# Two transposing filter loads, placed later on SyncE's queue, in a two-layer SSM-convolution and GeGLU kernel

## The chip, the cores and the metric

The kernel runs on one core of one Trainium2 chip. The metric is the device time of one execution in microseconds, the median of several runs; lower is better. Engines are named as in the profile: PE is TensorE's matmul, PEld its weight load, DVE is VectorE, ACT is ScalarE, POOL is GpSimd, SP is SyncE, which here only issues DMA transfers.

## What is computed

The input x has 2048 tokens of 576 values in bf16. Two layers follow each other, each a gated long convolution and a GeGLU feed-forward block, with the same weights in both layers:

```python
x = A_q
x = x + _A_ref(_layernorm(x), A_k, A_v, A_shift_k, A_ssm_k, A_ssm_D)
x = x + _B_ref(_layernorm(x), B_w_gate, B_w_up, B_w_down)
x = x + _A_ref(_layernorm(x), A_k, A_v, A_shift_k, A_ssm_k, A_ssm_D)
x = x + _B_ref(_layernorm(x), B_w_gate, B_w_up, B_w_down)
```

`_A_ref(q, ...)` forms kv, a four-tap causal filter of k times v, convolves every channel of kv along the tokens with its filter ssm_k of 2048 taps (576 rows in memory, one per channel), adds kv times a constant and multiplies by q. `_B_ref` is (gelu(x w_gate) * (x w_up)) w_down with an inner width of 4608.

## The kernel before, in words

**Chunks and units.** Tokens are cut into four chunks of 512. A unit is one layer of one chunk. The convolution of a chunk doesn't depend on x and is computed once for both layers; it is done by blocks of 512 taps, so that chunk m needs the filter blocks 0 to m. Block b of ssm_k must be turned, since it lies channel by channel in memory and the matmuls want taps on partitions. Blocks 0 and 1 are loaded plainly (tile hn) and turned by PE (L1251). Blocks 2 and 3 are turned by the DMA itself: `natural(b)` (L1082) issues one transposing load from memory into half of a tile nat (L1086, 128 x 4 x 576 bf16, 576 KB) and then a store of that half into a memory buffer hs[b] (L1087). hs[2] and hs[3] are read by POOL's loads L239, at 124.3 and 312.0 us in the profile. The tile nat is one of two buffers of the pool "x" (tag x); the other holds x_c[0], the fp32 residual of chunk 0. x_c[1], first written by a gate at L892, needs a buffer of this pool.

**The set-up** (L1089 to L1479) prepares chunk 0: kv, the first convolution, the layernorms, and the turned rows xnT of unit (0,0). Its steps are tasks of a planner (`Plan`, L72): `add(engine, cost, function, dependencies)` enters a task; `order` simulates the engines, and the tasks are emitted by planned start. SP's tasks form the list `loads`, made a strict sequence by `chain` (L1464): x's first chunk, the filter block 1, gate/up tiles 0 and 1, `natural(2)`, gate/up tile 2. `load_x(1)`, the load of x's second chunk into the single buffer x_b (pool xbp), is a POOL task (L1472) after `pluses`, the four gates on DVE (L1394) that read x's first chunk out of that buffer.

The end of the set-up, for each of the four row groups j of chunk 0: ACT makes yh (L1385), DVE gates (L1394), ACT squares (L1411, with an accumulator read), POOL makes ve and rstd (L1419, L1420), DVE normalises to xn (L1427), PE turns xn (L1439, L1441), DVE or ACT copies the turned rows to xnT (L1446, L1449). Forty filler matmuls (L1366) run on PE in the wait. Then the first gate/up matmuls start in halves of their columns (L1008, tile ps in the profile). Beside its roots, POOL issues the loads of k's and v's second chunk (L229, L234) and stores the transformed filter and kv blocks (Hd at L1270, Kd at L1296).

**After the set-up** (L1483) SP gets the w_down tiles 0 and 1, `natural(3)`, and w_down tile 2. Then the loop over visits runs (L1500): a visit is a third of the inner width for one unit, 12 gate/up tiles (4 tiles of weights per load, so three loads a visit) and then four groups of down matmuls (L1577). Between the tiles, `fill` works off the convolution of later chunks by costs. Gate/up weights stand in three buffers: the load of group n+3 is queued when group n is used up. Each engine and each DMA queue works in the order of emission.

Of the kernel before, what the change touches and what calls it, by code (L numbers as in the profile page):

```python
# [25 lines left out]
FG = 4  # L26
# [45 lines left out]
class Plan:  # L72
# [8 lines left out]
    def add(self, eng, cost, run=None, deps=(), lat=0.0, bank=False, frees=(), ready=0.0, prio=0.0):  # L81
        task = Task(eng, cost, run, [d for d in deps if d is not None], lat, bank, list(frees), ready, prio)
        for b in task.frees:
            b.users += 1
        self.tasks.append(task)
        return task
# [607 lines left out]
def ssm_geglu_kernel(ctx, tc, A_q, A_k, A_v, A_shift_k, A_ssm_k, A_ssm_D, B_x, B_w_gate, B_w_up,  # L694
                     B_w_down, out):
    nc = tc.nc
# [42 lines left out]
    def run_late(limit):  # L739
        if not late or late[0][0] > t.pe or max(t.dve, t.pe - 1.0) + C_EVD > limit:  # L740
            return False
        add_late()
        return True
# [42 lines left out]
    def load_wd(n):  # L786
        if n >= NWB * 2:
            return
        r0 = (n % (NP * 2)) * WT * P
        d = dpool.tile([P, WT, D], BF16, tag="wd", name="wd")  # L790
        nc.sync.dma_start(out=d[:], in_=B_w_down[r0:r0 + WT * P, :].rearrange("(ft p) d -> p ft d", p=P))
        wd[n] = d

    def load_x(c, eng=None):
        x_b[c] = xbp.tile([P, RT, D], BF16, name=f"x_b{c}", tag="xb")
        (eng or nc.gpsimd).dma_start(out=x_b[c][:],
                                     in_=q2[c * CH:(c + 1) * CH, :].rearrange("(p j) d -> p j d", j=RT))
        xb_at[c] = t.pe + 8.0
# [175 lines left out]
    def run_vq(limit):  # L974
        if not vq:
            return False
        need, cost, run = vq[0]
        if isinstance(need, float):
            r = need
        elif need[0] == "v":  # L980
            r = need[1].get(need[2], NEVER)
        else:
            r = NEVER if len(xn_made) >= 3 or not xn_open() else need[1].get("rstd_at", NEVER)
        if r > t.pe + 0.2 or max(t.dve, t.pe - 1.0) + cost > limit:
            return False
        vq.popleft()
        run()
        t.on_dve(cost, r)
        return True
# [3 lines left out]
    def spreads(now=False, tensor=False):  # L993
        while xn_made and (now or xn_made[0][3] <= t.pe):
            if tensor and xn_made[0][0] == ahead[1] and t.pe > ahead[0] - SLOW and conv.ps_free[0] <= t.pe:
                turn_row(*xn_made.popleft())
                continue
            ui, j, xn, _, entry = xn_made.popleft()
            entry[0] = True
            if j == 0:  # L1000
                xnT_of[ui] = xtp.tile([P, NKC, CH], BF16, tag="xnT", name="xnT")
            spread(xnT_of[ui], j, xn)
            xn_done[ui] = j + 1
# [37 lines left out]
    def when_due(when, load, n):  # L1041
        due.append((when, len(due), load, n))
        due.sort(key=lambda d: d[0])

    def weights():

        while due:
            near = xn_made or (vq and isinstance(vq[0][0], tuple) and vq[0][0][0] == "xn")
            if near and due[0][0] > t.pe + HOLD:
                break  # L1050
            _, _, load, n = due.pop(0)
            load(n)
# [3 lines left out]
    def pressing():  # L1056

        ui = coming[0]
        return (ui is not None and xn_done.get(ui, 0) < RT and units[ui][1] in conv.z_at and bool(vq)
                and t.pe > due_at[0] - PRESS)  # L1060

    def fill(limit, tensor, conv_first):
        weights()
        conv.run_loads()
        spreads(tensor=tensor)
        while True:
            if run_late(limit):
                continue
            if conv_first:
                if not (conv.run_v(limit) or run_vq(limit)):  # L1070
                    break
            elif not (run_vq(limit) or not pressing() and conv.run_v(limit)):
                break
        run_aq(min(limit, t.pe + 2.3))
        if tensor:
            for _ in range(3):
                if pressing() and (units[coming[0]][1], RT - 1) in conv.y_at or not conv.run_p():
                    break
# [3 lines left out]
    def natural(b):  # L1082
        if not nat:
            nat.append(xpool.tile([P, 2, RT, D], BF16, tag="x", name="nat"))
        h = nat[0][:, b - 2, :, :]
        nc.sync.dma_start_transpose(out=h, in_=A_ssm_k[:, b * BS:(b + 1) * BS])  # L1086
        nc.sync.dma_start(out=conv.hs[b].rearrange("(r p) d -> p r d", p=P), in_=h)  # L1087

    with tc.manual_schedule():  # L1089
# [5 lines left out]
        add = plan.add  # L1095
        with ExitStack() as es:
# [48 lines left out]
            def chain(tasks):  # L1145
                for a, b in zip(tasks, tasks[1:]):
                    b.deps.append(a)
# [135 lines left out]
            for m in KTS:  # L1283
                K0[m] = []
                for s in range(2):
                    def fill_ps(task, m=m, s=s):
                        if s == 0:
# [4 lines left out]
                                           prio=-4.0 * KTS.index(m)))  # L1292
# [71 lines left out]
            def busy():  # L1364
                for _ in range(4):
# [5 lines left out]
            loads = [add("SP", 0.6, lambda: load_x(0, nc.sync)),  # L1371
                     add("SP", 1.2, lambda: hn.__setitem__(1, load_hn(1)))]
# [7 lines left out]
            early_xn, pluses, copies = [], [], {}  # L1380
# [77 lines left out]
            for n in range(3):  # L1458
                loads.append(add("SP", 2.0, lambda n=n: load_wgu(n), [[], [], t0][n]))
                loads[-1].lat = 6.0  # L1460
                if n == 1:
                    loads.append(add("SP", 6.0, lambda: natural(2)))
            wg0 = loads[2]
            chain(loads)  # L1464
            add("ACT", 1.28, lambda: nc.scalar.activation(out=warm[:], in_=conv.pis[:], func=ACT.Gelu_apprx_tanh), [tsin], prio=20.0)
            for fi in range(2):
# [2 lines left out]
                    turn[fi] = task.slot  # L1469
                    gu_half(early[fi], fi, 0)  # L1470
                later(lambda me: add("PE", 0.99, me(half_of), early_xn[0] + early_xn[1] + [wg0], bank=True, prio=0.0))
            add("POOL", 0.6, lambda: load_x(1), pluses, prio=-50.0)  # L1472
            order = plan.order({"DVE": 1.9, "ACT": 3.3, "PE": 3.0, "POOL": 3.0, "SP": 4.5})
            for task in order:
                task.run()
# [4 lines left out]

        hpool = pool("hT", 1)
        dpool = pool("wd", 3)
        for n in range(2):  # L1483
            load_wd(n)
        natural(3)
        load_wd(2)
        conv.step(1, loaded=True)
        conv.left = len(conv.V)
        for m in range(2, NCH):
# [10 lines left out]
        for at, (wb, ph, ui, first, final) in enumerate(visits):  # L1500
# [33 lines left out]
            for fi in range(FP):  # L1534
                n, gi = divmod(wb * FP + fi, FG)
                w = wgu[n]
                if wb == 0 and fi in early:
                    pair = early.pop(fi)
                    taken[0] += 1
                    gu_half(pair, fi, 1)  # L1540
                    t.pe = max(t.pe, free.popleft()) + C_GU / 2
                else:
                    pair = pr("gu")
                    gu(pair, w, gi, lambda a: a, xnT)
                    t.pe = max(t.pe, free.popleft()) + C_GU
                while run_late(NEVER):
                    pass
                if hurry() and t.act <= t.pe + 0.2:
                    ga = work.tile([P, 2, CH], BF16, tag="ga", name="ga")
                    nc.scalar.activation(out=ga[:, 0, :], in_=pair[:, 0, :], func=ACT.Gelu_apprx_tanh)  # L1550
                    nc.scalar.copy(out=ga[:, 1, :], in_=pair[:, 1, :])  # L1551
                    nc.vector.tensor_tensor(out=hT[:, fi, :], in0=ga[:, 0, :], in1=ga[:, 1, :], op=ALU.mult)  # L1552
                    there = t.on_act(2 * C_GELU, max(t.pe + 0.15, gone[0]))
                    gone.append(t.on_dve(C_HB, there + 0.15) + 0.1)
                    free.append(there + 0.1)
                    bank_at[taken[0] % 3] = free[-1]
                    lead = FAR
                else:
                    ga = work.tile([P, CH], F32, tag="ga", name="ga")
                    nc.scalar.activation(out=ga[:], in_=pair[:, 0, :], func=ACT.Gelu_apprx_tanh)  # L1560
                    nc.vector.tensor_tensor(out=hT[:, fi, :], in0=ga[:], in1=pair[:, 1, :], op=ALU.mult)  # L1561
                    gone.append(t.on_dve(C_HT, t.on_act(C_GELU, max(t.pe + 0.15, gone[0])) + 0.15) + 0.1)
                    free.append(gone[-1])
                    bank_at[taken[0] % 3] = free[-1]
                    lead = LEAD
                if gi == FG - 1 and final:
                    when_due(t.pe + (FP - FG) * C_GU + 12.0, load_wgu, n + 3)
                fill(t.pe + C_GU + lead, hurry(), conv.left > 0)
            ahead[:] = [t.pe + RT * FP * C_DN, visits[at + 1][2] if at + 1 < len(visits) else None]
            for j in range(RT):  # L1570
# [105 lines left out]
```

## Time and profile before

| | us |
|---|---|
| median of 3 timed runs (937.97, 940.51, 940.17) | 940.17 |
| profiled execution | 937.94 |
| its span, first to last instruction | 936.2 |
| PE busy in the span | 920.4 |
| DVE / ACT / POOL busy | 580.1 / 325.7 / 140.3 |
| mean granted clock of TensorE | 0.994 |

All times of instructions below count from the start of the span. In the lines of the timeline the first number is the start, the second the duration, both in microseconds; after them come engine, line and operation, the tile written and the tile read, and in brackets the idle time of the engine before it with what ended it. A q behind an engine's name is its queue: an instruction that issues a transfer. The duration of such an instruction is how long the engine was busy issuing; the time from issue to landing is shown in the views of a tile and of the DMA queues. In the chain of waits, "issue" is time in which the profile shows nothing that was waited for.

### The profile page before, as it was taken

Reading aid. Unit: us, or ns where it says so; the run is one execution under the profiler, and the core shown is the slowest. Engines: PE = TensorE matmul, PEld = TensorE weight load, DVE = VectorE, ACT = ScalarE, POOL = GpSimd, SP = SyncE. Lnnn points to the kernel's source line nnn. Section 1 sums busy time; section 2 is a strip of 40 time slices with the busy share of each in tenths; the row PEclk is TensorE's granted clock in tenths of the full one; section 3 lists DMA queues with packets and bytes.
Section 4 is the critical chain, followed back from the end, with each engine's and each line's share of the span. In section 5 each row is a group of like instructions: output and inputs, shape, how many; then the busy total and the mean of one; then the engine's idle time right before and its main releaser. Section 6 shows DMA issues by size and latency. Waiting matters only on the chain.

```text
span 936.2 us, 19163 instructions
## 1 busy us (share of the span) xinstructions
PE 920.4 (98%) x8103; PEld 531.9 (57%) x8103; DVE 580.1 (62%) x1109; ACT 325.7 (35%) x594; POOL 140.3 (15%) x306
## 2 busy tenths in 40 slices
PE   9799999999999999999999999999999999999998
PEld 6555565665655646646556556556556556556555
DVE  7667677778788899758988973553333334533332
ACT  7546426553323136353222322451221214411211
POOL 3213200422012203230111200130000002100000
PEclk9989999999999999999999999999999999999999
DMA  9999998525934910891962920691630630696630
GB/s 234 144 249 234 309 243 186 138 52 167 222 119 91 262 48 2 171 310 40 217 191 75 190 78 26 102 204 26 130 99 2 128 102 14 121 221 152 147 70 27
DMA packets 125307, 129.69 MB, mean 139 GB/s; under 512 B 39714, under 2 KB 117411, under 8 KB 125220
## 3 DMA queue, kind: packets, MB, share of 16 engines
q1 hardware_dynamic: 115874, 92.33, 47.6%
q0 software_dynamic: 9200, 35.54, 12.3%
q8 instruction: 63, 1.03, 0.5%
q10 hardware_dynamic: 146, 0.59, 0.2%
q14 instruction: 24, 0.20, 0.1%
HBM read 108.09 MB, written 11.80 MB: 128 GB/s over the span
## 4 chain that ended last, share of the span: by engine, by line
PE 95%; DVE 2%; ACT 1%; issue 1%; POOL 1%; DMA 0%; ACTq 0%; DVEq 0%; SPq 0%
PE gu L1008 60%; PE dn L1577 28%; PE ps L281 1%; PE cps L290 1%; PE cps L343 1%; PE ps L1008 1%; PE ps L1218 1%; DVE kc L602 1%; PE cps L301 0%; PE ps L1340 0%; PE ps L1251 0%; DVE ab L308 0%; DVE cd L308 0%; ACT eo L303 0%; DMA xnT<-xn 0%
## 5 line engine op out<-in xcount | busy, mean ns | idle before, releaser
L1008 PE MATMUL gu<-xnT,wgu 64*128 64x512 bf16 x5148 | 561.1, 376 | 2.2 <-DVE x_c L1619 1.5
L1008 PEld LDWEIGHTS <-wgu 64*128 64x128 bf16 x5220 | 256.0, 94 | 305.2 <-issue 9.6
L1560 ACT ACTIVATE ga<-gu 128x512 f32<-128x512 f32 x256 | 152.8, 597 | 471.3 <-PE gu L1008 465.2
L1561 DVE TENSOR_TENSOR hT<-ga,gu 128x512 bf16<-128x512 f32 x256 | 175.6, 686 | 204.1 <-ACT ga L1560 202.6
L1577 PE MATMUL dn<-wd,hT 128*128 128x288 bf16 x2304 | 294.1, 286 | 0.0
L1577 PEld LDWEIGHTS <-hT 128*128 128x128 bf16 x2304 | 223.5, 98 | 65.4 <-issue 9.3
L840 POOL TENSOR_SCALAR means<-s 128x1 f32<-128x1 f32 x28 | 11.8, 422 | 239.9 <-DVE x_c L1613 205.3
L1621 DVE TENSOR_TENSOR x_c<-x_c,dn 128x576 f32<-128x576 f32 x32 | 24.1, 752 | 30.9 <-PE dn L1577 30.9
L1619 DVE SCALAR_TENSOR_TENSOR x_c<-dn,means,x_c 128x576 f32<-128x576 f32 x28 | 22.7, 815 | 26.8 <-PE dn L1577 26.7
L856 POOL TENSOR_TENSOR rstd<-ve,neghalf_t 128x1 f32<-128x1 f32 x56 | 35.5, 635 | 4.7
L320 DVE TENSOR_TENSOR prod<-prod 128x576 bf16<-128x576 bf16 x72 | 33.0, 458 | 2.5
L1550 ACT ACTIVATE ga<-gu 128x512 bf16<-128x512 f32 x30 | 17.9, 597 | 44.1 <-PE gu L1008 43.0
L303 ACT ACTIVATE eo<-cps 128x576 f32<-128x576 f32 x32 | 20.4, 649 | 25.0 <-DVE ab L308 9.8
L418 POOL DMA_DIRECT2D kr<-Kd x24 | 13.2, 550 | 87.3 <-DVE prod L319 86.1
L1600 DVE TENSOR_TENSOR xn<-x_c,dn 128x576 bf16<-128x576 f32 x15 | 11.3, 753 | 24.0 <-PE dn L1577 23.9
L602 DVE TENSOR_TENSOR kc<-ab,cd 128x288 bf16<-128x288 f32 x64 | 25.7, 451 | 0.0
L422 POOL DMA_DIRECT2D hr<-Hd x36 | 19.4, 540 | 41.1 <-DVE prod L319 39.5
L1552 DVE TENSOR_TENSOR hT<-ga 128x512 bf16<-128x512 bf16 x31 | 13.1, 422 | 18.5 <-ACT ga L1551 18.5
L840 POOL TENSOR_SCALAR nm<-s 128x1 f32<-128x1 f32 x28 | 8.7, 312 | 99.8 <-DVE x_c L892 99.7
L848 ACT ACTIVATE junk<-x_c,nm 128x576 bf16<-128x576 f32 x28 | 21.5, 767 | 4.9 <-POOL nm L840 4.9
L882 ACT ACTIVATE yh<-y,rstd 128x576 f32<-128x576 bf16 x28 | 21.4, 768 | 2.3 <-POOL rstd L856 2.3
L855 POOL TENSOR_SCALAR ve<-ss 128x1 f32<-128x1 f32 x56 | 15.3, 273 | 42.9 <-ACT junk L848 42.8
(170 smaller groups left out, 612.8 us busy)
## 6 DMA issues: line engine op xcount, KB each, us to landing
wgu<-in_B_w_gate_dram SPq DMA_DIRECT2D x45, 576.0 KB, 6.1
wd<-in_B_w_down_dram SPq DMA_DIRECT2D x30, 864.0 KB, 8.0
wgu<-in_B_w_up_dram SPq DMA_DIRECT2D x45, 512.0 KB, 8.2
hr<-Hd POOLq DMA_DIRECT2D x36, 288.0 KB, 7.8
kr<-Kd POOLq DMA_DIRECT2D x24, 288.0 KB, 6.6
Kd<-kc POOLq DMA_DIRECT2D x12, 288.0 KB, 6.4
k<-in_A_k_dram POOLq DMA_DIRECT2D x3, 1008.0 KB, 11.8
wgu<-in_B_w_up_dram SPq DMA_DIRECT2D x45, 64.0 KB, 8.0
```

What stands on the lines that cost most here:

```text
L320: nc.vector.tensor_tensor(out=dst[:, cols], in0=pr[:, 0, cols], in1=pr[:, 1, cols], op=ALU.subtract if part == 0 else ALU.add)
L602: nc.vector.tensor_tensor(out=into[k][:, plane, cols], in0=a, in1=b, op=op)
L840: nc.gpsimd.tensor_scalar(out=v["nm"][:], in0=v["s"][:], scalar1=-1.0 / D, scalar2=None, op0=ALU.mult)
L848: nc.scalar.activation(out=junk[:], in_=get_x(), func=ACT.Square, bias=v["nm"][:, 0:1], accum_out=v["ss"][:])
L856: nc.gpsimd.tensor_tensor(out=v["rstd"][:], in0=ve[:], in1=neghalf_t[:, 0:1], op=ALU.pow)
L882: nc.scalar.activation(out=g["yh"][:], in_=conv.y[c][:, j, :], func=ACT.Identity, scale=g["rstd"][:, 0:1], bias=1.0)
L1008: nc.tensor.matmul(cols(pair[:, s, :]), lhsT=w[r0:r0 + HK, k, gi * P:(gi + 1) * P], rhs=cols(xnT[r0:r0 + HK, blk_of[k], :]), start=(k == 0 ...
L1560: nc.scalar.activation(out=ga[:], in_=pair[:, 0, :], func=ACT.Gelu_apprx_tanh)
L1561: nc.vector.tensor_tensor(out=hT[:, fi, :], in0=ga[:], in1=pair[:, 1, :], op=ALU.mult)
L1577: nc.tensor.matmul(acc[:, h, 0:HW], lhsT=hT[:, fi, j * P:(j + 1) * P], rhs=wd[2 * wb + fi // WT][:, fi % WT, h * HW:(h + 1) * HW], start=( ...
L1619: nc.vector.scalar_tensor_tensor(out=xh, in0=acc[:, :, 0:HW], scalar=m_[:, 0:1], in1=xh, op0=op, op1=ALU.add)
L1621: nc.vector.tensor_tensor(out=xh, in0=xh, in1=acc[:, :, 0:HW], op=ALU.add)
```

## The change

Three moves on the DMA queues; no arithmetic is touched.

- In the set-up, `natural(2)` goes from between gate/up tiles 1 and 2 to the end of SP's sequence.
- `load_x(1)` goes from POOL to SP, behind gate/up tile 2 and ahead of `natural(2)`. It still waits for the four gates (`pluses`).
- `natural(3)` goes from between the w_down tiles 1 and 2 into the first visit, behind the matmuls of its ninth gate/up tile (`fi == 2 * FG`, FG = 4). The three w_down loads now stand together.

```diff
             for n in range(3):
                 loads.append(add("SP", 2.0, lambda n=n: load_wgu(n), [[], [], t0][n]))
                 loads[-1].lat = 6.0
-                if n == 1:
-                    loads.append(add("SP", 6.0, lambda: natural(2)))
             wg0 = loads[2]
+            loads.append(add("SP", 0.6, lambda: load_x(1, nc.sync), pluses, prio=-50.0))
+            loads.append(add("SP", 0.1, lambda: natural(2)))
             chain(loads)
...
-            add("POOL", 0.6, lambda: load_x(1), pluses, prio=-50.0)
             order = plan.order({"DVE": 1.9, "ACT": 3.3, "PE": 3.0, "POOL": 3.0, "SP": 4.5})
...
-        for n in range(2):
+        for n in range(3):
             load_wd(n)
-        natural(3)
-        load_wd(2)
         conv.step(1, loaded=True)
...
                     when_due(t.pe + (FP - FG) * C_GU + 12.0, load_wgu, n + 3)
+                if wb == 0 and fi == 2 * FG:
+                    natural(3)
                 fill(t.pe + C_GU + lead, hurry(), conv.left > 0)
```

## The prediction

> **What bounds the kernel.** Page, parts 1 and 2 first: TensorE (PE) is busy 98% of the span, so only time in which PE waits or runs at a lower clock can be won. The list of waits by engine gives PE 6.1 us in one wait, for DVE xn L1427, and under 1.6 us in every other. It lies in the set-up. The chain of waits there:
>
> ```profile
> 37.63 0.04 issue
> 37.67 2.41 PE ps L1366 x40
> 40.08 3.16 issue
> 43.24 0.28 POOL v L234
> 43.52 0.49 issue
> 44.01 0.54 POOL Kd L1296
> 44.55 0.02 issue
> 44.57 0.25 POOL ve L1419
> 44.82 0.07 issue
> 44.89 0.57 POOL rstd L1420
> ...
> 51.45 3.96 PE ps L1008 x36
> 55.41 1.00 PE ps L1251 x10
> ```
>
> PE ends its filler matmuls (L1366) at 40.08 and has nothing to do: the rows xn of chunk 0 need rstd, and POOL makes rstd only after it has issued two transfers at 43.24 and 44.01. The squares that rstd needs were there long before: ACT's first accumulator read (L1411) ends at 36.25, the last at 39.99. So POOL is what is late. Its timeline:
>
> ```profile
> 28.87 0.54 POOL L1270 DMA_DIRECT2D Hd<-h  x1 [1.43 <-ACT h L1267]
> 43.24 0.54 POOL L234 DMA_DIRECT2D v<-in_A_v_dram  x1 [13.83 <-issue]
> 44.01 0.54 POOL L1296 DMA_DIRECT2D Kd<-kc  x1 [0.23 <-issue]
> ```
>
> For 13.83 us POOL stands before the load of v's second chunk. The buffer of v was free at 29.9 (PE's last L275). What fits is another landing: that load is POOL's ninth transfer; the first, k's second chunk, was issued at 16.23 and by its tile's view took 26.4 us, so it landed at 42.6, 0.6 before v was issued. POOL's tenth transfer (Kd, 44.01) follows the landing of the second (Hd, 18.49 + 25.0 = 43.5) by 0.5. POOL does not issue a transfer while the one eight before it is in flight. And k was slow because of its neighbour on SyncE's (SP's) queue:
>
> ```profile
> 10.92 2.79 SPq L783 DMA_DIRECT2D wgu<-in_B_w_up_dram  x1
> 13.76 26.94 SPq L1086 DMA_TRANSPOSE nat<-in_A_ssm_k_dram  x1
> 51.12 0.40 SPq L1087 DMA_DIRECT2D hs<-nat  x1
> ...
> 57.31 11.32 SPq L1086 DMA_TRANSPOSE nat<-in_A_ssm_k_dram  x1
> 70.61 0.38 SPq L1087 DMA_DIRECT2D hs<-nat  x1
> ```
>
> The transposing load of filter block 2 (576 KB) holds SP 26.94 us and lands after 37.3; that of block 3 takes 11.32 and 13.3 (the two landings have the median 25.3 on the page). Beside the first ran k and seven stores of Hd and Kd (288 KB each, landing after 21.6 to 25.0 us, or up to 23.8); beside the second POOL issued nothing. The page's median for k's loads from POOL is 11.8 us. The last view is the busy time by stretches (PE, PEld, DVE, ACT, POOL, then PEclk, DMA share, GB/s):
>
> ```profile
> 42.00:44.00 2.00, 0.00 (x0) 0.00 (x0) 0.00 (x0) 0.00 (x0) 0.54 (x1) 1.00 1.09 193
> 46.00:48.00 2.00, 1.87 (x16) 1.36 (x16) 1.08 (x3) 0.43 (x1) 1.83 (x5) 0.50 1.31 88
> 52.00:54.00 2.00, 2.00 (x22) 1.46 (x20) 0.25 (x1) 0.00 (x0) 0.00 (x0) 0.50 1.02 398
> 56.00:58.00 2.00, 2.00 (x29) 1.42 (x29) 0.76 (x1) 0.20 (x1) 0.00 (x0) 1.00 1.14 202
> ```
>
> After the idle time the granted clock is 0.50 from about 45 to 55: the hole is paid twice.
>
> **The change, part by part.**
>
> *Block 2's transposing load leaves 13.76.* In its place SP issues the third gate/up tile (1152 KB), whose buffer is free since PE's L1251 at 9.4. No trace shows k beside that tile. From below, k takes the median 11.8 and lands at 28.0; from above it takes 26.4 as now. The nearest rows are the gate/up pieces issued up to 13.8, which land after 11.5 to 19.6; with the longest, k lands at 35.8. I take about 33. Between k's landing and the first root stand 0.6 to v, v 0.54, 0.23, Kd 0.54: 1.9 us. The first square is there at 36.25, so k costs nothing up to 34.4, and after that a microsecond for each.
>
> *The rows then.* The first rstd can be made from 36.3 and xn follows 0.92 after its ve (44.57 to 45.49), but DVE's last gate ends at 39.1: xn at 39.1 to 39.7. The last square (39.99) and roots 1.04 apart put the fourth xn at 41.5 to 42.1. PE's filler ends at 40.06; the transposes need banks that ACT's two copies of y (39.89, 1.16 long) free at 40.5 and 41.05. So the first of four turns starts at 40.6. A turn is 10 transposes, 1.04 us at full clock (L1251 at 36.45); four take 4.2, and the gate/up halves start at 44.8 instead of 51.39: **6.6 us**. Without the wait for banks it would be 7.1; with turns as slow as now (46.13 to 51.39, 5.26) 5.5.
>
> *The clock.* PE's pause shrinks from 6.07 us to about half a microsecond, so I expect no drop. The first 36 half matmuls, 3.96 us in the chain, then cost what the later 18 cost at full clock (1.09), twice: 2.18. **1.8 us**; nothing if the clock drops all the same.
>
> *Load of x's second chunk, POOL to SP.* On POOL it stood behind the roots (48.53, 0.63): nothing is gained there. On SP it waits for DVE's last gate, which frees x_b, until 38.9; behind it stand block 2's load, its store, the three w_down tiles and the next gate/up tiles. It lands 7.1 to 7.3 later, before now.
>
> *Block 2 at 39.5.* No row shows it beside x_b, v and Kd, the neighbours it may meet. From below 13.3 us as block 3, from above 37.3. POOL issues no transfer of its own then until the Hd stores (73.20 now, some 65 then), so the nearer row is 13.3: landed at 52.8. Then the store, and the first w_down tile at 53.3, landing after 7.3 to 15.0: 68.3 at the latest. The first down matmul (82.72) is due at 82.72 - 8.4 = 74.3. Hidden, with 6 us to spare.
>
> *Block 3 behind the ninth tile.* It takes 11.32 us of SP out from before the third w_down tile and stands behind the fifth gate/up tile (waiting for tile 8's release, 73.4 - 8.4 = 65.0, and 6.4 to issue): 71.4. Landing at 84.7 by its own row; behind it waits the sixth gate/up tile, issued at 85.1 and landing 15.7 later (median of set-up pieces), 100.8. It is due at the ninth tile of the next visit, 99.12 + 8 x 1.95 - 8.4 = 106.3. Hidden by 5.5 us. Its store is read at 312. The tile nat shares its slots with x_c; the next x_c is first written at 161.17, long after.
>
> Sum: 6.6 + 1.8 = **8.4 us** (5.5 to 8.9). From 51.45 to 168 the chain runs through PE alone and PE's later waits are 1.5 us at most, fed by PE's own results; the rest should shift as a whole. The profiled execution took 937.94 (span 936.2): 929.5. The median of the three timed runs, 940.17, lies 2.2 above it; with half of that I forecast **931**.
>
> **The rivals.**
>
> *k still late* (0.12): the wide gate/up tile holds k beyond 34.4. For it: it has twice the bytes of nat, and no row shows the pair. Against: k's own median 11.8. With k at 37 to 40, 2.6 to 5.6 us of the gain are gone: 934 to 937.
>
> *Bytes, not transposing* (0.04): a transposing load has no price of its own, k waits for what is queued, and the new neighbour has 576 KB more. A plain load of 576 KB (x_b) takes 7.3 us, so k lands at 49.9 instead of 42.6, and everything behind comes later by as much: about 947. Against: block 3's 13.3 us with no POOL transfer beside it, and the stores that needed 21.6 to 25.0 us. [...]
>
> *A slow transpose in the new place* (0.06; the one that makes it slower): beside POOL's Hd stores (73.20 and 85.67 now, 65 and 77 then) block 3 takes 37.3 us again. Then it lands at 108.7, the sixth gate/up tile at 124.8, 18.5 us after 106.3: 931 + 18.5 = 949. It decides from a landing at 90.2 (106.3 less 15.7 and 0.4), 18.8 us after the issue. For it: block 2's row now. Against: four stores are half the traffic that stood beside block 2.
>
> *Given back, or nothing* (0.06): the hole stays for a reason that I don't see, or a later stage is bound by something that doesn't shift, such as the preparation of the second unit, where the chain leaves PE (168 to 177). 937.5 to 940.
>
> **How the numbers follow.** The forecast has 0.72, with 928 to 934 of its own; the rivals 0.12, 0.04, 0.06 and 0.06. Range 927.5 to 937: the forecast and nearly all of the late k. A measurement of this kernel tells about 0.3% (2.8 us) from no change. Faster by more 0.84 (forecast and late k), within 0.06, slower 0.10 (bytes and the slow transpose).
>
> **What would show it.** Right: POOL issues v near 30 to 35 and the first rstd near 37; PE's wait for xn under 1 us; gate/up halves at 44 to 45.5 and granted clock 1.00 from 40 to 60; block 2 landed before 55; no wait of PE for wd or wgu. Wrong: v after 40, clock 0.50 between 45 and 55 again, or PE waiting for a weight tile between 74 and 125.

## The result and the profile after

The kernel after the change takes 929.46 us (median, 928.66 to 929.87), the kernel before 940.34 beside it (937.97 to 946.74): ratio 0.987, 95% interval 0.984 to 0.990, faster. The profiled execution takes 928.66, span 926.9 where before had 936.2: 9.3 us less. TensorE (PE) is busy 917.0 us, 99% of the span, and the mean granted clock is 1.000 where it was 0.994. The medians lie 10.9 us apart, more than the profiled executions, because that of the kernel before (937.94) is as short as the fastest of its six runs. Intervals here leave out the runs of the kernel before that lie more than 1.5% above its fastest, so that some ratios lie nearer to 1 than the medians suggest.

The views that answer to those of the prediction. POOL's timeline (start, duration, what; in brackets the idle time ahead and what ended it):

```profile
30.61 0.54 POOL L234 DMA_DIRECT2D v<-in_A_v_dram  x1 [0.74 <-PE ps L275]
31.28 0.54 POOL L1296 DMA_DIRECT2D Kd<-kc  x1
36.80 0.22 POOL L1419 TENSOR_SCALAR ve<-ss 128x1 f32<-128x1 f32 x1 [4.99 <-ACT junk L1411]
```

v's load no longer waits 13.83 us for a landing but 0.74 us for its buffer, and the first ve waits for ACT's squares, not for POOL. k, issued at 16.69, lands 11.1 us later, at 27.8. The chain of waits at the place where PE stood 6 us before:

```profile
40.44 0.53 ACT y L1404
...
41.02 0.38 PE ps L1441 x4
...
44.10 2.07 PE ps L1008 x36
46.17 1.00 PE ps L1251 x10
```

The four turns (PE turns the rows xn of the four row groups) take 41.02 to 44.10, then the gate/up halves begin. PE's largest wait here is 0.5 us, for ACT's copies of y (L1404), which free the banks. The matmuls of L1251 start at 46.17 where they started at 55.41, 9.24 earlier: 7.35 by the earlier halves (44.10 for 51.45) and 1.89 by their clock (2.07 for 3.96). That is the whole 9.3 us; nothing behind it gives any back. By stretches (PE, PEld, DVE, ACT, POOL, PEclk, DMA share, GB/s) the clock stays up:

```profile
42.00:44.00 2.00, 2.00 (x29) 1.45 (x26) 1.54 (x3) 1.66 (x2) 0.14 (x1) 1.00 1.15 245
46.00:48.00 2.00, 2.00 (x32) 1.55 (x28) 0.76 (x1) 0.00 (x0) 0.00 (x0) 1.00 0.73 239
```

And SyncE's (SP's) own queue:

```profile
39.32 0.33 SPq L796 DMA_DIRECT2D x_b<-in_A_q_dram  x1
39.70 3.59 SPq L1086 DMA_TRANSPOSE nat<-in_A_ssm_k_dram  x1
45.58 0.41 SPq L1087 DMA_DIRECT2D hs<-nat  x1
...
66.46 8.59 SPq L1086 DMA_TRANSPOSE nat<-in_A_ssm_k_dram  x1
77.01 0.38 SPq L1087 DMA_DIRECT2D hs<-nat  x1
```

Its store waits for nat, so its start tells the landing: block 2 lands 5.9 us after its issue (37.3 before), block 3 after 10.5 (13.3).

### The profile page after: what moved, and what is told of

Its sections match the earlier page's. It is cut to its first block, busy times and chain, and to the rows that moved or that the text cites. A ratio compares the mean times of both kernels' runs of the same rounds, so it can differ in the third digit from the quotient of the medians.

```text
span 926.9 us, 19167 instructions
## 1 busy us (share of the span) xinstructions
PE 917.0 (99%) x8103; PEld 529.8 (57%) x8103; DVE 579.7 (63%) x1109; ACT 325.7 (35%) x594; POOL 139.9 (15%) x305
## 3 DMA queue, kind: packets, MB, share of 16 engines
q8 instruction: 63, 1.03, 0.5%
## 4 chain that ended last, share of the span: by engine, by line
PE 95%; DVE 2%; ACT 1%; issue 0%; DMA 0%; POOL 0%; ACTq 0%; DVEq 0%; SPq 0%
PE gu L1008 60%; PE dn L1576 28%; PE ps L281 1%; PE cps L290 1%; PE cps L343 1%; PE ps L1218 1%; DVE kc L602 1%; PE cps L301 0%; PE ps L1008 0%; PE ps L1340 0%; PE ps L1251 0%; DVE ab L308 0%; DVE cd L308 0%; ACT eo L303 0%; DMA xnT<-xn 0%
## 5 line engine op out<-in xcount | busy, mean ns | idle before, releaser
L840 POOL TENSOR_SCALAR means<-s 128x1 f32<-128x1 f32 x28 | 11.8, 421 | 237.7 <-DVE x_c L1612 205.3
L303 ACT ACTIVATE eo<-cps 128x576 f32<-128x576 f32 x32 | 20.4, 650 | 25.0 <-DVE ab L308 9.8
L1599 DVE TENSOR_TENSOR xn<-x_c,dn 128x576 bf16<-128x576 f32 x15 | 11.3, 752 | 24.0 <-PE dn L1576 23.9
## 6 DMA issues: line engine op xcount, KB each, us to landing
k<-in_A_k_dram POOLq DMA_DIRECT2D x3, 1008.0 KB, 11.1
```

The costliest lines, as they stand in the source:

```text
L840: nc.gpsimd.tensor_scalar(out=v["nm"][:], in0=v["s"][:], scalar1=-1.0 / D, scalar2=None, op0=ALU.mult)
```

## The experiments

Theory T: a transposing load in flight beside POOL's transfers is slow and makes them slow; the old place of block 2 put it beside k and seven stores. The roots (ve and rstd on POOL) then come late. Rivals: its bytes or its place in SP's order are what matters (B); POOL's order alone is to blame (P); the clock, not the late roots, carries the gain (C); block 3's move brings part of it (M). "Before" beside the first eight runs below took 940.82 or 940.88 (median), beside the four last, with stores moved to ACT or SP, 938.79 and 938.97.

**A plain load in block 2's old place.** The kernel before, with rows of x in place of filter block 2, so that this kernel leaves out the turned block:

```
-        nc.sync.dma_start_transpose(out=h, in_=A_ssm_k[:, b * BS:(b + 1) * BS])
+        if b == 2:
+            nc.sync.dma_start(out=h, in_=q2[0:BS, :].rearrange("(p j) d -> p j d", j=RT))
+        else:
+            nc.sync.dma_start_transpose(out=h, in_=A_ssm_k[:, b * BS:(b + 1) * BS])
```

> The kernel before with block 2's transposing load replaced, in its old place, by a plain load of the same 576 KB into the same tile (rows of x, so filter block 2 holds other data; nothing else differs). Theory (it is the transposing that slows its neighbours): k lands after 10 to 16 us, v is issued at 30 to 33, no hole on PE; 929 to 932. Rival (bytes in SP's queue hold k, transposing or not): k lands after 22 us or more, v at 39 or later; 936 to 941.

929.27 us (928.53 to 932.73), ratio 0.987 [0.983, 0.991]. The profile of this run, SP's queue:

```profile
14.44 0.59 SPq L1087 DMA_DIRECT2D nat<-in_A_q_dram  x1
30.12 0.39 SPq L1090 DMA_DIRECT2D hs<-nat  x1
```

The same 576 KB in the same place, issued in 0.59 us and landed after 15.6, and k lands after 12.0, not 26.4. With nothing moved the whole gain is there. B falls as far as bytes and the place in SP's order go: the price is that of the transposing load. By the records of single packets that load is 2304 packets of 256 bytes, the plain one 128 of 4608; whether the turning or the small packets cost the time was not tested.

**Block 3 back, and block 2 back.** Each from the kernel after:

```
-        for n in range(3):
+        for n in range(2):
             load_wd(n)
+        natural(3)
+        load_wd(2)
...
-                if wb == 0 and fi == 2 * FG:
-                    natural(3)
```

> The changed kernel with block 3's load put back between w_down tiles 1 and 2; block 2 stays behind the load of x's second chunk. Theory: block 3's move is worth nothing by itself, it only keeps block 3 from standing in front of a w_down tile that isn't due before 73; 929 to 930.5. Rival (two transposing loads close together bring the trouble back, or w_down tile 2 is late): over 931.

929.2 us (927.34 to 929.54), ratio 0.991 [0.988, 0.994]: as after, 929.46. M falls; block 3's move is worth nothing here and does no harm.

```
                 loads[-1].lat = 6.0
+                if n == 1:
+                    loads.append(add("SP", 6.0, lambda: natural(2)))
             wg0 = loads[2]
             loads.append(add("SP", 0.6, lambda: load_x(1, nc.sync), pluses, prio=-50.0))
-            loads.append(add("SP", 0.1, lambda: natural(2)))
```

> The changed kernel with block 2's load put back between gate/up tiles 1 and 2; x's second chunk stays on SP and block 3 behind the ninth tile. Theory: the whole loss is back: k lands after 25 to 27 us, v is issued at about 43, PE waits 5 to 6.5 us for xn, granted clock 0.50 from 45 to 55; time 938 to 941. Rival (the other two moves carry a part of the gain): 931 to 936.

939.23 us (931.3 to 945.55), ratio 0.997 [0.994, 1.000]: with block 2 back in its old place the gain is gone in the median. The profiled execution is an exception (span 929.5): there k took 18.7 us and landed at 34.3, just early enough, and v was issued at 34.88, 0.56 behind it:

```profile
15.67 0.76 POOL L229 DMA_DIRECT2D k<-in_A_k_dram  x1
...
34.88 0.54 POOL L234 DMA_DIRECT2D v<-in_A_v_dram  x1 [6.03 <-PE ps L1340]
```

So the loss in the old place is no fixed price: k took 18.7 here and 26.4 in the profile of before, and the executions spread over 14 us, those of the kernel after over 1.2.

**Block 2 alone, without the wait behind x's load.** The kernel before, with block 2 behind the third gate/up tile; the dependence on the gates only places it last in the order of SP, it makes no instruction wait:

```
-                if n == 1:
-                    loads.append(add("SP", 6.0, lambda: natural(2)))
             wg0 = loads[2]
+            loads.append(add("SP", 0.1, lambda: natural(2), pluses, prio=-50.0))
```

> Only block 2's load is moved, to directly behind the third gate/up tile: x's second chunk stays on POOL, block 3 stays behind w_down tile 1. On SP nothing makes block 2 wait for the gates now, so it issues at about 24.4, as soon as the third gate/up tile is issued. Theory (POOL does not issue a transfer while the one eight before it is in flight, and k was slow because a transposing load ran beside it): k is nearly through by then (in the changed kernel it landed at 27.8), v is issued at 31 to 34, the roots start at 37 to 38, gate/up halves start at 44 to 46; time 929 to 932. Rival (what counts is that block 2 waits for the gates until 39, clear of the Hd and Kd stores): the transposing load catches k's tail and the first Hd store, v or the last Kd goes out after 38, and half or more of the gain is gone; 934 to 940.

935.17 us (928.16 to 940.24), ratio 0.993 [0.989, 0.997]: half the gain. Block 2 is issued at 19.43 and lands 36.8 us later; k, issued before it, lands after 11.3, so POOL is as early as in after, and the turns end at 44.51. Block 2 stands behind a gate/up tile on SP's queue, and its first packet moves only at 33.21. The transfers of POOL that had landed by 34.02 are as fast as in after (six stores in at most 9.8 us, there 9.9); the last Hd store, v and the last Kd store, in flight after that, land after 11.0, 23.1 and 23.7 us, where after has 5.9, 7.2 and 7.3. So within one execution POOL's transfers are slow while block 2's packets move, and not before. But then, in the chain of waits of this run:

```profile
44.53 0.77 DVE xnT L1446
45.30 7.63 issue
52.93 4.02 PE ps L1008 x36
```

"issue" is time in which PE waits for nothing that the profile shows. The operands are there: the turned rows since 45.30, the last pieces of gate/up tiles 0 and 1 since 18.0 and 24.3. What is missing are PE's instructions. Of the DMA queues between 24 and 46 us (packets, MB, share of 16 engines) q8 brings instructions; in after:

```profile
q8 instruction: 2, 0.03, 0.7%
```

in this run the list goes on from q1 to q14:

```profile
q1 hardware_dynamic: 2669, 1.32, 52.7%
q14 instruction: 1, 0.01, 0.1%
```

q8 has no line, so not one packet. Over the whole run q8 moves 63 packets and 1.03 MB, which makes some 64 bytes for each of PE's 16,206 instructions and some 256 instructions for a packet of 16 KB (an estimate, which takes all of q8 as PE's). In the records of single packets after has one of 16 KB at 35.01 and the next at 44.79; this run has one at 21.00 and then none until 48.77. It took 2.65 us, to 51.42, and PE went on at 52.93.

**The same with 60 PE instructions fewer ahead** (10 filler matmuls for 40, each with its weight load), to test that reading: if instructions are short, PE must get exactly that much further.

```
-                for _ in range(4):
+                for _ in range(1):
                     nc.tensor.matmul(held["y", 1][:, 1, 384:512], lhsT=ident[:], ...)
```

> e1 (block 2 alone moved, not waiting for the gates) with 10 instead of 40 filler matmuls, so 60 instructions fewer on PE ahead of the gate/up halves. In e1, PE and its weight load stopped together after one weight load of L1008, with all transfers that L1008 needs landed; the instruction queue q8 had moved no packet between 24 and 46. Theory (PE had no instructions, since the transposing load held up the transfer that brings them): in a profile in which that transfer is late again, PE now gets some 30 matmuls of L1008 further before it stops, and resumes just after the packet. Rival (L1008 waits for data): PE stops again at the first matmul of L1008. Time as e1, 928 to 941; if the packet is in time in this profile, nothing is told.

932.7 us (930.01 to 940.43), ratio 0.997 [0.992, 1.002]. The chain of waits:

```profile
44.82 1.75 PE ps L1008 x30
46.57 3.09 issue
49.65 0.51 PE ps L1008 x6
```

30 half matmuls, each with its weight load, are 60 instructions; then PE stops in the middle of an accumulation until the packet, at 45.62 for 2.67 us, has come. So a third party besides POOL and SP pays for the transposing load: PE's own instruction stream. It does not pay each time: in the profile of before the packet came at 36.17, in the midst of block 2's packets.

**POOL's order alone.** The kernel before, with v's load and the last Kd store behind the four roots in POOL's order, so that nothing in POOL stands before the roots:

```
-            add("POOL", 0.6, lambda: conv.load_v(1, nc.gpsimd), [x for m in KTS for x in K0[m]], prio=-20.0)
...
+            behind = [add("POOL", 0.6, lambda: conv.load_v(1, nc.gpsimd), [x for m in KTS for x in K0[m]] + roots, prio=-20.0)]
+            behind.append(add("POOL", 0.55, lambda: nc.gpsimd.dma_start(out=conv.Kd[0][3], ...), K0[3] + behind, prio=-30.0))
...  (the load of x's second chunk stands behind both)
```

> The kernel before with all transposing loads where they were; on POOL the load of v's second chunk and the last Kd store are put behind the four roots. Theory: the roots no longer stand behind a transfer that waits for k, though k is as slow as before (about 26 us); rstd from 36.8, gate/up halves at 44 to 45, no clock drop; 929 to 932, perhaps up to 2 us more where the third gate/up tile (issued at 51.6, landing near 62 to 64) is late for the ninth tile at 64. Rival (rows xn are late for another reason than the order on POOL, such as traffic on the DMA engines): no gain, 938 to 941.

936.58 us (929.34 to 938.98), ratio 0.995 [0.992, 0.998]. The roots are ready from 35.82, and the place of PE's wait only changes. DVE's timeline:

```profile
46.86 0.76 DVE L1253 COPY ht<-ps 128x1152 bf16<-128x1152 bf16 x1 [6.12 <-DMA Hd<-h]
```

The copy writes a buffer that the first Hd store still reads; the store took 28.80 us from issue to landing. PE's instruction packet came late here too, at 48.89. P is right that POOL's order was the first thing in the way, and wrong that it was the only one.

**Late roots without a slow transfer.** The kernel after, with 11 idle operations of 7.59 us in all on POOL ahead of the first root; then the same with three times the filler matmuls, which keep PE busy to 45.5 us; from 44 to 52 us the granted clock is 0.50 in the first and 1.00 in the second.

```
+                    if j == 2:
+                        pad = tmp.tile([P, 1], F32, name="pad")
+                        for _ in range(11):
+                            nc.gpsimd.tensor_tensor(out=pad[:], in0=ve[:], in1=neghalf_t[:, 0:1], op=ALU.pow)
...  (second kernel only)
-                for _ in range(4):
+                for _ in range(12):
```

> The changed kernel with all transfers where they are, but eleven idle pow instructions on POOL between the first ve and the first rstd (some 6.5 to 8 us), so that rstd is late without any transfer being slow. Theory (late roots alone make the loss of the kernel before, and the lower clock comes from PE's pause): turns start at 44.5 to 46.5 instead of 41.0, granted clock 0.50 for some 10 us; 935 to 939.5. Rival (the loss before came mainly from slow transfers elsewhere): under 934.

> As g1, with 120 instead of 40 filler matmuls on PE, so that PE is busy until about 45 while it waits. Theory: the granted clock stays at 1.00 and the second price is saved: 2 to 4 us less than g1, 932.5 to 936. Rival (the clock does not hang on the pause): as g1.

936.55 us (935.94 to 938.38) and 935.26 (933.47 to 936.27), ratios 0.999 [0.996, 1.003] and 0.997 [0.994, 1.001]. One stretch of each by engine; first the one with little filler, then the other:

```profile
46.00:48.00 2.00, 1.94 (x16) 1.37 (x16) 1.08 (x3) 0.52 (x1) 1.83 (x5) 0.50 0.47 162
```

```profile
46.00:48.00 2.00, 1.46 (x17) 0.95 (x18) 1.08 (x3) 0.83 (x2) 1.91 (x4) 1.00 0.01 1
```

Late roots alone bring back 7.1 us of the loss, with every transfer fast. Holding the clock at 1.00 wins only 1.3 of them, less than the 2 to 4 that was expected: the same 16 or 17 transposes fit into the stretch at either clock, since roots 1.04 apart and DVE's copies pace them (POOL is busy 1.83 and 1.91 us of this stretch, DVE 1.90 and 2.00 of the next). In the gate/up halves behind the turns the clock counts, 3.00 us against 2.07 (0.68 and 1.00 granted from 52 to 54); in the kernel before, where it stayed at 0.50 through all of them, they took 3.96:

```profile
51.38 3.00 PE ps L1008 x36
```

```profile
50.76 2.07 PE ps L1008 x36
```

C falls as the main cause.

**Who the neighbour is.** The kernel before with the eight stores issued by ACT behind its own copies, then with k's and v's loads on ACT as well; block 2 stands where it stood in SP's order.

```
-                add("POOL", 0.55, lambda: nc.gpsimd.dma_start(out=conv.Hd[0][m], ...), outs, prio=-30.0)
+                add("ACT", 0.1, lambda: nc.scalar.dma_start(out=conv.Hd[0][m], ...), outs, prio=-30.0)
...  (and the same for Kd; in the second kernel for load_k and load_v)
```

> The kernel before with the set-up's eight stores of Hd and Kd issued by ACT, right behind the copies that make them, in place of POOL; k's and v's loads stay on POOL, block 2 and 3 stay in their old places. It tells apart what makes a transposing load and its neighbours slow. Theory A, any transfers beside it: block 2 still lands after more than 25 us (before 37.3), the stores after more than 15. POOL then has only two transfers, so v never waits for a transfer eight before it; the halves start near 44 to 46 unless PE's instructions or a store's buffer come late, and the time lies anywhere between 929 and 938. Theory B, the neighbours must come from POOL's queue: with one such transfer (k) beside it, block 2 lands after at most 20 us, the stores after at most 10, k after about 12; 929 to 932, and some microseconds more if ACT's own issuing holds up its copies.

> As the run with the stores on ACT, with k's and v's second chunks loaded by ACT too, so that POOL issues nothing until x's second chunk behind the roots. Theory A, any transfers beside the transposing load: block 2 still lands after more than 25 us, k after more than 18. Theory B, only POOL's queue: block 2 lands after at most 16 us (13.3 for block 3 before, with nothing of POOL beside it), k after about 12; 928 to 932, and more if ACT's issuing holds up its copies.

928.94 us (927.74 to 929.54) and 929.53 (927.66 to 929.96), ratios 0.990 [0.987, 0.992] and 0.990 [0.988, 0.993]: the gain of the change, with no load moved in the order. But the transposing load was not issued where it was before. SP's queue, and the list of waits, of the first:

```profile
24.79 5.10 SPq L1086 DMA_TRANSPOSE nat<-in_A_ssm_k_dram  x1
34.85 0.41 SPq L1087 DMA_DIRECT2D hs<-nat  x1
```

```profile
SPq L1086 <- DMA wgu<-in_B_w_up_dram: 11.3, 1, 11.3
```

It waited 11.3 us for an earlier gate/up piece, a wait that the kernel before does not have. The instruction records of the trace tell why. The instruction that issues a transfer names a semaphore, on which the trace then has the landing (16 events for each of POOL's 111 transfers in the kernel before), and in none of the fourteen traces is a transfer issued before the last one on its semaphore has landed, as far as landings are on record. SP and ACT share eight such semaphores; here block 2 follows that piece on one of them. POOL has eight of its own and uses them strictly in turn, so v follows k, 0.56 us behind its last landing event at 42.68: that is the wait of 13.83 us in the kernel before. The limit of eight that the prediction found thus goes with the eight semaphores that the traces show for POOL. Block 2 lands after 10.0 us (at most 11.8 in the second kernel), the stores after 9.4 at most. Since lateness alone might do that, a pair: block 2 behind the third gate/up tile and behind one Hd store that SP issues near 26 us, the other seven stores on POOL, then on ACT.

```
-                if n == 1:
-                    loads.append(add("SP", 6.0, lambda: natural(2)))
             wg0 = loads[2]
+            loads.append(add("SP", 0.4, lambda: nc.sync.dma_start(out=conv.Hd[0][KTS[2]], ...), H0[KTS[2]], prio=-50.0))
+            loads.append(add("SP", 0.1, lambda: natural(2), prio=-50.0))
...  (that store no longer on POOL; in the second kernel the other seven on ACT)
```

> First of a pair that differs in one thing, who issues seven stores. The kernel before, with block 2's transposing load behind the third gate/up tile and, between the two, the third store of Hd moved from POOL to SP: that store waits for its rows (written near 26 us), so that the transposing load is issued near 26 as in the two runs with ACT's stores, where it came late because it stood waiting for a gate/up piece. The other stores stay on POOL; block 3 and x as before. If POOL's queue is what makes a transposing load slow (it landed after 10.0 and 11.8 us beside ACT's stores), block 2 lands after more than 20 us here, beside the last Hd store, the last Kd stores and v, which land after more than 12. If the lateness alone had made it fast, block 2 lands after at most 14, and the stores after at most 10. The time is not what this run is for: 928 to 937.

> Second of the pair: as the first, with the other seven stores of Hd and Kd issued by ACT in place of POOL; PE's, DVE's and SP's order are the same. If POOL's queue is what makes a transposing load slow, block 2, again issued near 26, lands after at most 14 us and the stores after at most 10, where the first of the pair has more than 20 and 12. If it is the lateness alone, both of the pair agree within 3 us. 928 to 933.

928.96 us (927.99 to 934.83) and 931.09 (930.69 to 933.94), ratios 0.991 [0.987, 0.994] and 0.993 [0.990, 0.995]. SP's queue of the first:

```profile
26.23 15.10 SPq L1086 DMA_TRANSPOSE nat<-in_A_ssm_k_dram  x1
56.35 0.40 SPq L1087 DMA_DIRECT2D hs<-nat  x1
```

and its transfers issued between 24 and 40 us (KB each, median us to landing):

```profile
Hd<-h POOLq DMA_DIRECT2D x1, 288.0 KB, 20.4
...
nat<-in_A_ssm_k_dram SPq DMA_TRANSPOSE x1, 30.1
```

In the same stretch of the kernel with all stores on ACT:

```profile
Hd<-h ACTq DMA_DIRECT2D x2, 288.0 KB, 6.3
...
nat<-in_A_ssm_k_dram SPq DMA_TRANSPOSE x1, 10.0
```

So lateness alone does not make the load fast: issued at 26.23, later than the 24.79 with ACT's stores, it needs 30.1 us beside POOL's transfers, and Hd and v land after 20.4 and 20.7. One Kd store of POOL's, issued at 28.06, landed after 6.4 where more than 12 was expected. The second of the pair is a partial miss: its transposing load again stood waiting, this time for the landing of an ACT store, and came out at 31.18, not near 26:

```profile
31.18 6.42 SPq L1086 DMA_TRANSPOSE nat<-in_A_ssm_k_dram  x1
45.97 0.41 SPq L1087 DMA_DIRECT2D hs<-nat  x1
```

It landed by 45.97, within 14.8 us where at most 14 was expected; its stores took up to 13.4 where 10 was.

These times from issue to landing hold a part in which block 2 only stands behind SP's gate/up pieces. The records of single packets show when its 2304 packets moved, and how many MB of POOL's (queue q0) and ACT's (q10) moved in that time:

| run | issued at | its packets, from to | us | MB beside it |
|---|---|---|---|---|
| before | 13.76 | 21.99 to 50.29 | 28.3 | 3.27 of POOL |
| POOL's roots first | 14.23 | 21.19 to 53.96 | 32.8 | 3.21 of POOL |
| block 2 alone | 19.43 | 33.21 to 55.58 | 22.4 | 1.46 of POOL |
| first of the pair | 26.23 | 34.15 to 55.72 | 21.6 | 1.41 of POOL |
| second of the pair | 31.18 | 34.53 to 45.02 | 10.5 | 0.25 of POOL, 0.59 of ACT |
| stores on ACT | 24.79 | 28.11 to 33.20 | 5.1 | 0.44 of ACT |
| stores and loads on ACT | 29.18 | 30.75 to 36.91 | 6.2 | 0.27 of ACT |
| after | 39.70 | 42.29 to 45.03 | 2.7 | none |

The packets of the pair start only 0.4 us apart, so in time it is a better pair than its issues suggest. But it also differs in how much moved beside block 2, and so do the two kernels with all stores on ACT, in whose stretch POOL moved nothing. Per MB beside it, block 2 lost some 8 to 14 us with POOL's transfers and 5 to 13 with ACT's (an estimate from the table: its time less the 2.7 us alone, divided by the MB). So it is shown that the load is slow where POOL's transfers move beside it and fast where nothing does. That POOL's queue is worse than ACT's for the same amount is not shown.

In the profiled execution of the first of the pair the slow load did no harm to the time: k had landed at 27.9 and PE's packet came at 39.92, in time. One of its four runs took 934.83.

## Why the prediction was right

It gave 931.0 with 927.5 to 937; 929.46 came. Of the profiled execution it expected 8.4 us; 9.3 were won. Point by point:

- **POOL stands for k's landing, and k is slow because of block 2.** Held: v issued 30.61, first rstd 37.11 (predicted 30 to 35, and 37). That k is slow because of block 2 is shown by the plain load in its place, and by block 2 put back. The wait for the transfer eight before is in line with all fourteen traces, in which POOL uses eight semaphores in turn.
- **k lands at about 33.** It landed at 27.8, by the lower bound of the two (28.0). The wide gate/up tile beside it costs k nothing, so the rival "k still late" has no ground; the 1.4 us of slack that I counted on were 6.6.
- **The first turn at 40.6 by the bank wait.** 41.02, with the wait for ACT's y as named; the set-up begins 0.46 later in this execution (L1293 at 30.35, 29.89 before), which is the difference.
- **A turn 1.04, four 4.2.** The mis-sized term: 3.08 for four. I priced it by L1251's ten transposes, of another tile; ten of a turn (8 of L1441 and 2 of L1439) take 0.73 at full clock. 1.1 us more were won than forecast, 0.4 lost by the start: 7.35 for 6.6.
- **The clock, 1.8 us.** 1.89 in these 36 halves, and 1.00 throughout. As a cause by itself it gives 1.3 in the pair with idle operations.
- **Block 2 landed at 52.8, block 3 13.3 after its issue.** 45.6, and 10.5. The prices were too high, and nothing hung on them. Block 2 in its new place met none of POOL's transfers: v and the last Kd, issued at 30.61 and 31.28, had landed by 38.58, before its issue at 39.70. PE's list of waits names no wd and no wgu down to 0.5 us. The slow transpose in the new place did not come about, but it was not put to the test either: the first two Hd stores had landed by 71.02, block 3's packets moved from 71.89 to 76.53, and the next stores were issued at 76.42 and 77.05. That they missed each other, by 0.9 us, is luck; the rival had block 3 beside four stores.
- **Bytes, not transposing.** Refuted by the plain load, which has the same bytes: in one place, the transposing load landed after 37.3 us and the plain one after 15.6. With nothing of POOL's beside it the transposing load was no slower than a plain one: in the kernel after block 2 landed after 5.9 us, v, of as many bytes, after 7.2.

What the prediction did not see: POOL was one victim of three. It took the eighth-transfer wait for the whole mechanism; by that, moving block 2 behind the third tile, or POOL's roots ahead of v, would have brought all of it. Each brought half or less (5.7 and 4.2 us in the medians), because in the executions that were profiled PE's instructions or a buffer behind a slow store came late instead. What the change does right lies in a detail that the prediction used only for a landing time: behind x's load, which waits for the gates until 39, block 2 starts when POOL's transfers are over. The prediction saw that POOL issues nothing then, but not that this is what makes the place good.

Open: why a transposing load and POOL's transfers slow each other down, whether it is the turning or the 256-byte packets, whether POOL's stores or its loads do it, and whether as much traffic from another queue would do the same. No version was found that is faster than after: after and four of the others that compute all of it lie between 928.9 and 929.6.

## What to carry to other kernels

Give a transposing load a place in which no other queue has transfers in flight (in every slow case here they were POOL's: its packets took 21.6 to 32.8 us beside them, 2.7 with none); a queue that is already waiting for the right moment is a cheap way to get it (here SP's, where x's load, issued at 39.32, waited for the gates). Read from the packets when a load moved: of the 36.8 us from issue to landing in "block 2 alone", 13.8 went by before the first packet. Before work on a late engine is put in a new order, look at the landing times around it: the stores of 288 KB issued from 10 to 45 us took 22.5 us (Hd) and 22.8 (Kd) in the median before, 8.0 and 7.8 after, and there moving one victim only uncovered the next. An "issue" wait of PE with all operands there (7.63 us in "block 2 alone") is to be compared with the packets of its instruction queue.

## What the runs showed of the hardware

- **Transposing load and POOL's transfers.** The 2304 packets of block 2's 576 KB took 21.6 to 32.8 us beside 1.4 to 3.3 MB of POOL's, 5.1 and 6.2 beside 0.4 and 0.3 MB of ACT's, and 2.7 with neither (the table above). From issue to landing that was 30.1 to 40.9 us, at most 11.8, and 5.9. Its issue held SP for 15 to 28 us in the first case and 3.6 to 5.1 in the others; the second of the pair lies between, 10.5 us and 6.4. Hd stores of 288 KB took up to 28.8 us beside it, k up to 30.3.
- **Eight transfers in flight.** In the fourteen traces POOL's transfers name eight semaphores in turn, and none is issued before the one eight before it has landed, as far as landings are on record (in the kernel before, v and the last Kd store 0.56 and 0.53 us behind it). SP's and ACT's share another eight: a load on SP waited 11.3 us when ACT was given stores.
- **Instructions come by DMA too, and can be late.** The profile lists a queue q8 of the kind "instruction", with 63 packets of 16 KB in a run. PE stood 7.6 and 3.1 us for one of them that came at 48.77 and 45.62, where the kernel after has it at 35.01.
- **A bad place for a transfer shows in the spread.** 927.6 to 951.7 us for the kernel before over the 56 runs of two comparisons, 928.66 to 929.87 for the kernel after over six.
